# A layer's tail at the end of one DMA stream: x added by a matmul, pieces moved up by one, the last piece cut into 96 and 32 rows

## The chip, the cores and the metric

One core of one Trainium2 chip. The metric is device time in microseconds, the median of several executions. A profile of one execution is shown beside it: engines PE (TensorE), DVE (VectorE), ACT (ScalarE), POOL (GpSimd), SP (SyncE), and the DMA queues.

## The reference

One decode step (batch 2, one token, width 512), float32. The input is normalised once; attention over the last 2048 cached positions with 32 heads of 128, and a bilinear feed-forward block, are both computed from it, and both are added to x.

```python
def _A_ref(x, k_cache, v_cache, wq, wo):      # B, Hq, Dh = 2, 32, 128; W = 2048
    q = (x @ wq) ...                           # per head
    k, v = k_cache[:, :, Sk - W:, :], v_cache[:, :, Sk - W:, :]
    scores = jnp.einsum("bhqd,bhkd->bhqk", q, k) * (Dh ** -0.5)
    p = _softmax(scores, axis=-1)
    o = jnp.einsum("bhqk,bhkd->bhqd", p, v)
    return o.transpose(...).reshape(B, Sq, Hq * Dh) @ wo

def _B_ref(x, w_gate, w_up, w_down):           # F = 1376
    h = (x @ w_gate) * (x @ w_up)
    return h @ w_down

xn = _layernorm(x, axis=-1)
return x + _A_ref(xn, ...) + _B_ref(xn, ...)
```

## The kernel before

All inputs are laid out in one DRAM array, `stream`, in the order in which they are used, and SyncE's DMA queue reads it from front to back. `loads()` is the table of this order. A load is a list of units: `k` and `v` of a head (128 x 4096), `wq` of a group of four heads, `wo` of a head, `wd` a piece of w_down (128 x 512 each: 128 of its 1376 rows, so pieces 0 to 9 are full and piece 10 has 96 rows and is filled up to 128 with zeros). Loads 1 to 22 go into three large buffers in turn (`step0` to `step2`), loads 0 and 23 into `extra`. Load 24 goes into `step0` in separate transfers, so that its units can be used as they land: v 31, wo 28 to 31, then w_down's pieces in three sizes.

A load is issued once the instructions that used its buffer's last content are done; the helper `put` derives these waits from overlapping areas, and `emit` writes all instructions in program order. Every instruction therefore has the line of `emit` in the profile (L199).

For each head VectorE multiplies the keys by q and sums (`score`), for each group of four heads `weights` makes the softmax weights, TensorE weighs the values (`weigh`, into `o_ps`), ScalarE copies them (`fold`), TensorE gathers the diagonal (`gather`, into `pk_ps`, shown as gu), VectorE scales it (`scaled`, into `oT`). The output row is summed in PSUM in two ways. `add_rows` is one matmul of 512 columns into one of four row pairs of `acc`; `add_groups` is four matmuls of 128 columns into `acc_g` (in the bank of q, shown as q). `wo` and `down` use them for wo and w_down; `hT` holds the feed-forward's hidden row, transposed, 128 of its entries a column. `turn` fills it during load 3.

At the end `acc` goes to `acc_sb` in SBUF, and a group of four matmuls with `id4` (a selection matrix: for j = 0 to 3 and b = 0, 1, entry b of row 32j + b is one) adds its four row pairs into `acc_g`. Then `acc_g` is copied to `o_out` and stored. x itself is loaded by ScalarE's DMA queue into two rows of `xr`, which GpSimd has cleared, and VectorE adds it where it copies `acc`.

Of the kernel before, what the change touches and what calls it, by code (L numbers as in the profile page):

```python
# [5 lines left out]
ALU = mybir.AluOpType  # L6
# [4 lines left out]
P = 128  # L11
B, D, H, DH, SK, F = 2, 512, 32, 128, 8192, 1376
# [7 lines left out]
NFC = F // P  # L20
FR = F - NFC * P
# [4 lines left out]
GROUPS = [list(range(g * HG, g * HG + HG)) for g in range(NG)]  # L26
N = B * HG
M = 4 * N
CK, CO = J * DH, D
CX = B * NC + 4 * N + 4 * HG + 2 * NFB + 2 + B  # L30
BUFS = 3
WIDTH = 13824
WIDTH_X = 4096


def loads():


    def units(kind, *ids):
        w = {"k": CK, "v": CK, "wo": CO, "wd": CO, "wq": HG * DH}[kind]  # L40
        return [(kind, i, w) for i in ids]

    def wq(g, *cs):
        return units("wq", *[(g, c) for c in cs])

    big = {
        1: units("k", 0, 1, 2),
        3: units("k", 3, 4) + units("v", 0),
        4: units("k", 5, 6) + units("v", 1),
        5: units("k", 7, 8) + units("v", 2),  # L50
    }
    k, v = 9, 3
    for n in range(6, 20):
        i = 1 + n % 2
        big[n] = units("k", *range(k, k + i)) + units("v", *range(v, v + 3 - i))
        k, v = k + i, v + 3 - i
    big[20] = units("k", 30, 31) + units("v", 24)
    big[21] = units("v", 25, 26, 27)
    big[22] = units("v", 28, 29)
    small = {  # L60
        1: wq(1, 0, 1, 2),
        3: wq(1, 3) + wq(2, 0, 1),
        4: wq(2, 2, 3) + units("wd", 0),
        5: wq(3, 0, 1, 2),
        6: units("wo", 0, 1, 2),
        7: wq(3, 3) + units("wo", 3) + wq(4, 0),
        8: units("wo", 4, 5, 6),
        9: units("wo", 7) + wq(4, 1, 2),
        10: wq(4, 3) + wq(5, 0, 1),
        11: units("wo", 8, 9, 10),  # L70
        12: units("wo", 11) + wq(5, 2, 3),
        13: wq(6, 0, 1, 2),
        14: units("wo", 12, 13, 14),
        15: units("wo", 15) + wq(6, 3) + wq(7, 0),
        16: units("wo", 16, 17, 18),
        17: units("wo", 19) + wq(7, 1, 2),
        18: wq(7, 3) + units("wd", NFC),
        19: units("wo", 20, 21, 22),
        20: units("wo", 23),
        21: units("wo", 26, 27),  # L80
        22: units("wo", 24, 25),
    }
    out = [
        (0, "x", [("c", 0, CX)] + wq(0, 0, 1, 2, 3)),
        (1, 0, big[1] + small[1]),
        (2, 1, [(w, 0, NC * F) for w in ("wg", "wu")]),
        (3, 2, big[3] + small[3]),
    ]
    for n in range(4, 23):
        out += [(n, (1, 0, 2)[(n - 4) % 3], big[n] + small[n])]  # L90
    out += [
        (23, "x", units("v", 30)),
        (24, 0, units("v", 31)),
        (24, 0, units("wo", 28, 29, 30, 31)),
        (24, 0, units("wd", 1, 2, 3, 4)),
        (24, 0, units("wd", 5, 6, 7)),
        (24, 0, units("wd", 8)),
        (24, 0, units("wd", 9)),
    ]
    return out  # L100
# [133 lines left out]
        return call  # L234


def build(nc, stream, x_nat, out):
    pr = Program(nc)
    pe, dve, act, pool = pr.pe, pr.dve, pr.act, pr.pool

    buf = [pr.sb(f"step{i}", [P, WIDTH]) for i in range(BUFS)]
    buf_x = pr.sb("extra", [P, WIDTH_X])
    xr = pr.sb("xr", [P, D])
    ones = pr.sb("ones", [P, P])
    mean_w = pr.sb("mean_w", [P, P])
    eps_t = pr.sb("eps", [P, 1])
    zero = pr.sb("zero", [P, 1])
# [5 lines left out]
    p_all = pr.sb("p", [P, 2, HG, JG, M])  # L253
    s_t = [pr.sb(f"s{i}", [P, HG, J]) for i in range(2)]
    mt = pr.sb("mt", [P, 32])
    mtt = pr.sb("mtt", [P, 32])
    mc = pr.sb("mc", [P, 1])
    both = pr.sb("both", [P, 4 * HG + N])
# [5 lines left out]
    hT = pr.sb("hT", [P, 4, NFB, B])  # L264
    acc_sb = pr.sb("acc_sb", [P, D])
# [4 lines left out]
    acc = pr.ps("acc", [P, FB])  # L270
# [4 lines left out]
    got, used, queue, pos = {}, {}, [], 0  # L275
    for n, t, fields in loads():
        tile = buf_x if t == "x" else buf[t]
        c0 = used.get(n, 0)
        for kind, i, w in fields:
            c = used.get(n, 0)  # L280
            got[kind, i] = tile[:, c : c + w]
            used[n] = c + w
        c1 = used[n]
        assert c1 <= tile.shape[1], (n, c1)
        src = stream[pos : pos + P * (c1 - c0)].rearrange("(p i) -> p i", p=P)
        pos += P * (c1 - c0)
        queue.append((n, tile[:, c0:c1], src))

    def issue(upto):
        while queue and queue[0][0] <= upto:  # L290
# [6 lines left out]
    dve.memset(ones, 1.0)  # L297
    for t in gu_ps + [acc]:
        dve.memset(t, 0.0)
    for t in (xr, zero, mt, both, p_all):  # L300
        pool.memset(t, 0.0)
    pr.load("ACT", xr[:B, :], x_nat)

    c0 = got["c", 0]
    dve.tensor_copy(cst, c0)
# [9 lines left out]
    id4 = cst[:, cut[4] : cut[5]]  # L315
# [82 lines left out]
    def weigh(h, bank=None, first=None, last=None):  # L398
        g, hh = divmod(h, HG)
        bank = g % 2 if bank is None else bank  # L400
        first = hh == 0 if first is None else first
        last = hh == HG - 1 if last is None else last
        v = got["v", h]
        for i in range(JG):
            j = 32 * (i % 4)
            pe.matmul(
                o_ps[bank][j : j + M, :], p_all[:, g % 2, hh, i, :],
                v[:, i * FB : (i + 1) * FB],
                start=(first and i < 4), stop=(last and i >= JG - 4),
            )  # L410
# [58 lines left out]
    def turn():  # L469
        dve.tensor_copy(  # L470
            hT.rearrange("p i n b -> p (i n b)"), hT_ps[:, 0 : 4 * B * NFB]
        )

    def down(c, add, *args, **kw):
        k = min(P, F - c * P)
        add(hT[:k, c % 4, c // 4, :], got["wd", c][:k], *args, **kw)

    def wo(h, add, *args, **kw):
        g, hh = divmod(h, HG)
        add(oT[g % 2][:, B * hh : B * hh + B], got["wo", h], *args, **kw)  # L480

    def keep_busy(lhsT, n):
        pe.matmul(
            spare[:M, : n * P], lhsT, xnb[:, :n, :].rearrange("p c k -> p (c k)"),
            start=True, stop=True,
        )
# [14 lines left out]
    for n, _, fields in loads():  # L501
        plan.setdefault(n, []).extend(fields)
# [19 lines left out]
    for n in range(3, 21):  # L522
# [13 lines left out]
        for c in has(n, "wd"):  # L536
            down(c, add_rows, 1)
# [31 lines left out]
    g = NG - 1  # L569
    a, b, c, d = GROUPS[g]  # L570
# [10 lines left out]
        weigh(h)  # L581
    for h in GROUPS[g - 1]:
        wo(h, add_rows, h % 2)
    weigh(d)
    keep_busy(p_all[:, g % 2, HG - 1, 0, :], 2)
    fold(g)
# [1 line left out]
    scaled(g)  # L588
    for h in GROUPS[g]:
        wo(h, add_rows, h % HG)  # L590
    for i in range(1, 5):
        down(i, add_rows, i % 4, last=True)
    dve.tensor_tensor(acc_sb, acc, xr, op=ALU.add)
    down(5, add_groups)
    add_groups(id4, acc_sb)
    for i in range(6, NFC):
        down(i, add_groups, last=(i == NFC - 1))
    dve.tensor_copy(o_out, acc_g)
    pr.load("SP", out, o_out)
# [3 lines left out]
def laid_out(x):  # L603

    import numpy as np

    a = x["A_x"].reshape(B, D)
    xs = np.zeros((P, CX), a.dtype)
    xs[:, : B * NC] = a.reshape(B, P, NC).transpose(1, 0, 2).reshape(P, B * NC)
    o = B * NC  # L610
    for r in range(4):
        for n in range(N):
            xs[4 * n + r :: 32, o + r * N + n] = 1.0
    o += 4 * N
    for n in range(HG):
        for q in range(4):
            xs[32 * q + n, o + 4 * n + q] = 1.0
    o += 4 * HG
    for n in range(NFB):
        for b in range(B):  # L620
            xs[32 * n + b, o + n * B + b] = 1.0
    o += 2 * NFB
    for j in range(4):
        for b in range(B):
            xs[32 * j + b, o + b] = 1.0
    xs[:, o + 2 :] = a[:, 0]
    cache = {
        kind: x[name][:, :, SK - W :, :].reshape(B, H, HB, J * DH).transpose(1, 0, 2, 3)
        for kind, name in (("k", "A_k_cache"), ("v", "A_v_cache"))
    }  # L630
    wq = x["A_wq"].reshape(P, NC, H * DH)
    wo = x["A_wo"].reshape(H, P, D)
    gu = {
        kind: x[name].reshape(P, NC * F)
        for kind, name in (("wg", "B_w_gate"), ("wu", "B_w_up"))
    }
    wd = x["B_w_down"]

    def field(kind, i):
        if kind == "c":  # L640
            return xs
        if kind in ("k", "v"):
            return cache[kind][i].reshape(P, CK)
        if kind == "wq":
            g, c = i
            return wq[:, c, g * HG * DH : (g + 1) * HG * DH]
        if kind == "wo":
            return wo[i]
        if kind == "wd":
            return np.pad(wd[i * P : (i + 1) * P], ((0, max(0, (i + 1) * P - F)), (0, 0)))  # L650
        return gu[kind]

    parts = [
        np.concatenate([field(kind, i) for kind, i, _ in fields], axis=1).ravel()
        for _, _, fields in loads()
    ]
    return {"stream": np.concatenate(parts), "x": a}


_INS = ["A_x", "A_k_cache", "A_v_cache", "A_wq", "A_wo", "B_w_gate", "B_w_up", "B_w_down"]  # L660
# [24 lines left out]
```

## Time and profile before

| | us |
|---|---|
| median of 3 runs | 377.14 |
| the runs | 376.97 to 377.26 |
| profiled execution | 377.09 |
| its span, first to last instruction | 375.8 |
| VectorE busy | 302.8 (81%) |
| TensorE matmul busy | 191.2 (51%) |
| ScalarE busy | 14.5 (4%) |

The profiled execution's time contains 1.29 us outside its span. Busy shares are averages over the span; the chain of waits, the timeline and the DMA queues say what was waited for at a given place.

### The profile page before, as it was taken

How to read it: one execution, taken by the hardware profiler on the slowest of the kernel's cores; microseconds unless marked ns; L12 is line 12 of the kernel's file. 1: busy time of each engine (PE TensorE's matmuls, PEld its weight loads, DVE VectorE, ACT ScalarE, POOL GpSimd, SP SyncE). 2: the span in 40 equal slices, each digit the busy share in tenths (PEclk: the TensorE clock that was granted, in tenths of full speed). 3: DMA queues.
4: the chain of work that ended last, by engine and by line, in shares of the span. 5: the costliest groups of instructions: out<-in, count | busy, mean ns of one | idle time of the engine just before them, and what ended most of it. 6: DMA issues, size and time to landing. Idle time of an engine off the chain costs nothing.

```text
span 375.8 us, 1953 instructions
## 1 busy us (share of the span) xinstructions
PE 191.2 (51%) x844; PEld 56.9 (15%) x844; DVE 302.8 (81%) x165; ACT 14.5 (4%) x28; POOL 2.6 (1%) x9
## 2 busy tenths in 40 slices
PE   1652646804654265617437263472657355243986
PEld 0210121101210011101121011110111012010322
DVE  4069979999999996999599399969969996999401
ACT  1000100000000000000100000000000001000100
POOL 2000000000000000000000000000000000000000
PEclk9956956676665658758555885856566685565889
DMA  9899989999899998999989999899999999999996
GB/s 398 377 469 413 471 377 471 408 436 466 383 465 418 436 461 383 465 424 430 465 384 459 424 430 465 388 461 418 430 459 414 429 453 434 430 414 411 424 419 242
DMA packets 4475, 159.73 MB, mean 425 GB/s; under 512 B 498, under 2 KB 626, under 8 KB 1012
## 3 DMA queue, kind: packets, MB, share of 16 engines
q1 hardware_dynamic: 4464, 159.62, 98.6%
q8 instruction: 6, 0.10, 0.1%
q14 instruction: 1, 0.01, 0.0%
q10 hardware_dynamic: 4, 0.00, 0.0%
HBM read 159.55 MB, written 0.07 MB: 425 GB/s over the span
## 4 chain that ended last, share of the span: by engine, by line
DVE 49%; DMA 47%; PE 2%; issue 0%; SPq 0%
DMA step<-in_stream_dram 47%; DVE s L199 24%; DVE step L199 23%; PE acc L199 1%; DVE both L199 1%; PE tr L199 1%; PE q L199 0%; SPq L199 0%; DVE mt L199 0%; DVE nm L199 0%; DVE mtt L199 0%; DVE mc L199 0%; DVE rec L199 0%; DVE oT L199 0%; DVE o_out L199 0%
## 5 line engine op out<-in xcount | busy, mean ns | idle before, releaser
L199 DVE TENSOR_TENSOR step<-step,q 128x4096 f32<-128x4096 f32 x32 | 141.1, 4409 | 38.0 <-DMA step<-in_stream_dram 37.9
L199 DVE TENSOR_REDUCE s<-step 128x32 f32<-128x4096 f32 x32 | 141.4, 4418 | 0.8
L199 PE MATMUL o_ps<-step,p 128*32 128x512 f32 x496 | 101.2, 923 | 68.1 <-DMA step<-in_stream_dram 66.5
L199 PE MATMUL q<-step,xnb 128*128 128x512 f32 x56 | 37.5, 801 | 28.7 <-DVE step L199 21.7
L199 PE MATMUL acc<-step,oT 128*2 128x512 f32 x64 | 23.5, 922 | 40.7 <-DVE oT L199 27.0
L199 PEld LDWEIGHTS o_ps<-step,p 128*32 128x32 f32 x496 | 21.2, 154 | 130.2 <-DMA step<-in_stream_dram 74.0
L199 PEld LDWEIGHTS q<-step,xnb 128*128 128x128 f32 x56 | 12.5, 251 | 55.0 <-DVE step L199 28.2
L199 ACT ACTIVATE p<-s,zero 64x128 f32<-64x128 f32 x16 | 6.4, 399 | 266.2 <-DVE s L199 266.1
L199 PE MATMUL tr<-both,ones 128*128 128x24 f32 (+1 forms) x18 | 4.7, 344 | 19.7 <-DVE both L199 19.7
L199 DVE TENSOR_TENSOR oT<-gu,rec 128x8 f32<-128x8 f32 x8 | 1.3, 159 | 14.8 <-PE gu L199 14.8
L199 PE MATMUL gu<-step,xn 128*2 128x512 f32 (+1 forms) x48 | 8.7, 659 | 7.5 <-DMA step<-in_stream_dram 7.5
L199 PE MATMUL gu<-cst,o_sb 128*128 128x8 f32 x64 | 10.1, 285 | 3.1 <-ACT o_sb L199 3.1
L199 PEld LDWEIGHTS gu<-cst,o_sb 128*128 128x128 f32 x64 | 9.4, 225 | 10.8 <-ACT o_sb L199 9.1
L199 PEld LDWEIGHTS acc<-step,oT 128*2 128x2 f32 x64 | 1.5, 82 | 51.5 <-DVE oT L199 27.7
L199 PEld LDWEIGHTS tr<-both,ones 128*128 128x128 f32 x18 | 3.7, 256 | 29.2 <-DVE both L199 29.2
L199 PE MATMUL q<-extra,xnb 128*128 128x512 f32 x8 | 6.4, 978 | 1.9 <-DVE xnb L199 1.9
L199 DVE TENSOR_REDUCE nm<-tr 64x4 f32<-64x8 f32 x16 | 2.6, 163 | 5.2 <-PE tr L199 5.1
L199 ACT COPY o_sb<-o_ps 128x512 f32<-128x512 f32 x8 | 4.7, 586 | 48.2 <-PE o_ps L199 48.2
L199 PE MATMUL gu<-cst,h_sb 128*128 128x6 f32 x8 | 1.9, 361 | 5.4 <-DVE h_sb L199 5.4
L199 PEld LDWEIGHTS gu<-step,xn 128*2 128x2 f32 x48 | 2.0, 93 | 14.9 <-DMA step<-in_stream_dram 9.1
L199 PE MATMUL tr<-st,mean_w 128*128 128x4 f32 x2 | 0.6, 366 | 6.5 <-DVE st L199 6.5
L199 DVE TENSOR_REDUCE both<-p 128x8 f32<-128x256 f32 x8 | 3.3, 414 | 0.6 <-ACT p L199 0.6
(50 smaller groups left out, 39.3 us busy)
## 6 DMA issues: line engine op xcount, KB each, us to landing
step<-in_stream_dram SPq DMA_DIRECT2D x17, 6912.0 KB, 31.3
step<-in_stream_dram SPq DMA_DIRECT2D x2, 6656.0 KB, 33.6
step<-in_stream_dram SPq DMA_DIRECT2D x1, 6400.0 KB, 29.5
step<-in_stream_dram SPq DMA_DIRECT2D x1, 5504.0 KB, 33.4
step<-in_stream_dram SPq DMA_DIRECT2D x1, 4608.0 KB, 23.8
extra<-in_stream_dram SPq DMA_DIRECT2D x1, 2048.0 KB, 28.3
step<-in_stream_dram SPq DMA_DIRECT2D x1, 2048.0 KB, 24.8
step<-in_stream_dram SPq DMA_DIRECT2D x2, 1024.0 KB, 19.6
```

Source lines behind the costliest of these rows:

```text
L199: ins = getattr(e, method)(*args, **kw)
```

## The change

x is no longer loaded by itself. Its two rows are stored in piece 10 of w_down, as rows 96 and 97 of the 128, and two rows of a unit matrix (from `id4`) are copied behind the 96 hidden entries in `hT`; the matmul of piece 10, now with 98 rows, adds x. `xr`, its memset, its load and its input are gone. `acc` is copied by ScalarE instead of added to by VectorE.

Piece 1 of w_down moves into load 22 and is used between the matmuls of wo for heads 24 and 25; load 24 has pieces 2 to 5 in one transfer, 6 and 7 in one, then 8, then 9. Pieces 2 to 5 are added by rows, 6 to 9 by groups, and the group with `acc_sb` comes behind piece 7 instead of piece 5.

Piece 9 is loaded in two transfers: rows 0 to 95, and rows 96 to 127 as four blocks of eight rows. In `stream` a row of padding is stored behind each block, so that the four blocks are a dimension of their own.

```diff
+LAST, LAST_K = 32, 4
...
-        22: units("wo", 24, 25),
+        22: units("wo", 24, 25) + units("wd", 1),
...
-        (24, 0, units("wd", 1, 2, 3, 4)),
-        (24, 0, units("wd", 5, 6, 7)),
+        (24, 0, units("wd", 2, 3, 4, 5)),
+        (24, 0, units("wd", 6, 7)),
         (24, 0, units("wd", 8)),
         (24, 0, units("wd", 9)),
...
-    xr = pr.sb("xr", [P, D])
...
+        if fields[0][:2] == ("wd", NFC - 1):
+            k, lo, j = LAST_K, P - LAST, LAST // LAST_K
+            src = stream[pos : pos + lo * CO].rearrange("(p i) -> p i", p=lo)
+            queue.append((n, tile[:lo, c0:c1], src))
+            pos += lo * CO
+            src = stream[pos : pos + k * (j + 1) * CO].rearrange(
+                "(i j d) -> i j d", i=k, d=CO
+            )
+            queue.append((n, tile[lo:, c0:c1], src[:, :j, :]))
+        else:
+            queue.append((n, tile[:, c0:c1], src))
         pos += P * (c1 - c0)
-        queue.append((n, tile[:, c0:c1], src))
...
-    for t in (xr, zero, mt, both, p_all):
+    for t in (zero, mt, both, p_all):
         pool.memset(t, 0.0)
-    pr.load("ACT", xr[:B, :], x_nat)
...
         )
+        dve.tensor_copy(hT[FR : FR + B, NFC % 4, NFC // 4, :], id4[FR : FR + B, :])
 
     def down(c, add, *args, **kw):
-        k = min(P, F - c * P)
+        k = min(P, F + B - c * P)
...
     for h in GROUPS[g - 1]:
         wo(h, add_rows, h % 2)
+        if h == GROUPS[g - 1][0]:
+            down(1, add_rows, 2)
...
-    for i in range(1, 5):
+    for i in range(2, 6):
         down(i, add_rows, i % 4, last=True)
-    dve.tensor_tensor(acc_sb, acc, xr, op=ALU.add)
-    down(5, add_groups)
+    act.copy(acc_sb, acc)
+    for i in (6, 7):
+        down(i, add_groups)
     add_groups(id4, acc_sb)
-    for i in range(6, NFC):
+    for i in range(8, NFC):
         down(i, add_groups, last=(i == NFC - 1))
```

TensorE's last instructions before the change, from the matmuls of wo's last four heads on; `s_d567` to `s_d571` are the landings of load 24's transfers behind v 31.

```order
L199 MATMUL acc<-step,oT 2x512 [waits s_d567,s_DVE]
L199 MATMUL acc<-step,oT 2x512 x3
L199 MATMUL acc<-step,hT 2x512 [waits s_d568]
L199 MATMUL acc<-step,hT 2x512 x3
L199 MATMUL q<-step,hT 2x128 [waits s_d569]
L199 MATMUL q<-step,hT 2x128 x3
L199 MATMUL q<-acc_sb,cst 2x128 [waits s_DVE]
L199 MATMUL q<-acc_sb,cst 2x128 x3
L199 MATMUL q<-step,hT 2x128 x8
L199 MATMUL q<-step,hT 2x128 [waits s_d570]
L199 MATMUL q<-step,hT 2x128 x3
L199 MATMUL q<-step,hT 2x128 [waits s_d571]
```

The same place after the change; here `s_d566` to `s_d571` are the landings.

```order
L200 MATMUL acc<-step,oT 2x512 [waits s_d566,s_DVE]
L200 MATMUL acc<-step,oT 2x512 x3
L200 MATMUL acc<-step,hT 2x512 [waits s_d567]
L200 MATMUL acc<-step,hT 2x512 x3
L200 MATMUL q<-step,hT 2x128 [waits s_d568]
L200 MATMUL q<-step,hT 2x128 x7
L200 MATMUL q<-acc_sb,cst 2x128 [waits s_ACT]
L200 MATMUL q<-acc_sb,cst 2x128 x3
L200 MATMUL q<-step,hT 2x128 [waits s_d569]
L200 MATMUL q<-step,hT 2x128 x3
L200 MATMUL q<-step,hT 2x128 [waits s_d570,s_d571]
```

The group with `acc_sb` now waits for ScalarE and stands behind two groups of `hT` instead of one; three groups of w_down stand ahead of the last piece instead of four, and the last piece waits for two landings.

SyncE's last transfers before the change.

```order
L199 DMA step<-in_stream_dram 128x9216 [waits s_DVE]
L199 DMA extra<-in_stream_dram 128x4096
L199 DMA step<-in_stream_dram 128x4096 [waits s_DVE]
L199 DMA step<-in_stream_dram 128x2048 [waits s_DVE]
L199 DMA step<-in_stream_dram 128x2048
L199 DMA step<-in_stream_dram 128x1536 [waits s_PE]
L199 DMA step<-in_stream_dram 128x512 [waits s_PE] x2
L199 DMA out_dram<-o_out 128x128 [waits s_DVE]
```

And after it.

```order
L200 DMA step<-in_stream_dram 128x9728 [waits s_DVE]
L200 DMA extra<-in_stream_dram 128x4096
L200 DMA step<-in_stream_dram 128x4096 [waits s_DVE]
L200 DMA step<-in_stream_dram 128x2048 [waits s_DVE]
L200 DMA step<-in_stream_dram 128x2048
L200 DMA step<-in_stream_dram 128x1024 [waits s_PE]
L200 DMA step<-in_stream_dram 128x512 [waits s_PE]
L200 DMA step<-in_stream_dram 96x512 [waits s_PE]
L200 DMA step<-in_stream_dram 32x1x512
L200 DMA out_dram<-o_out 128x128 [waits s_DVE]
```

Load 22 (the first row) has grown by 512 columns and the transfer of three pieces has lost as many; the last row of 128x512 has become one of 96 and one of 32 rows.

More of the change, by code (lines that the diff above doesn't have):

```diff
@@ L234, in __getattr__, with build @@
         return call
-def build(nc, stream, x_nat, out):
+def build(nc, stream, out):
     pr = Program(nc)
@@ L649, in field @@
         if kind == "wd":
-            return np.pad(wd[i * P : (i + 1) * P], ((0, max(0, (i + 1) * P - F)), (0, 0)))
+            rows = np.zeros((P, D), wd.dtype)
+            rows[: min(P, F - i * P)] = wd[i * P : (i + 1) * P]
+            if i == NFC:
+                rows[FR : FR + B] = a
+            return rows
         return gu[kind]
@@ L656, in laid_out @@
     ]
-    return {"stream": np.concatenate(parts), "x": a}
+    last = wd[NFC * P - LAST : NFC * P].reshape(LAST_K, LAST // LAST_K, D)
+    parts.append(parts.pop()[: -LAST * D])
+    parts.append(np.pad(last, ((0, 0), (0, 1), (0, 0))).ravel())
+    return {"stream": np.concatenate(parts)}
 _INS = ["A_x", "A_k_cache", "A_v_cache", "A_wq", "A_wo", "B_w_gate", "B_w_up", "B_w_down"]
```

## The prediction

> **What bounds the kernel now.** I read the page first: its span, the line of DMA shares, the DMA queues.
>
> ```profile
> span 375.8 us, 1953 instructions
> ...
> DMA  9899989999899998999989999899999999999996
> ...
> q1 hardware_dynamic: 4464, 159.62, 98.6%
> q8 instruction: 6, 0.10, 0.1%
> q14 instruction: 1, 0.01, 0.0%
> q10 hardware_dynamic: 4, 0.00, 0.0%
> HBM read 159.55 MB, written 0.07 MB: 425 GB/s over the span
> ```
>
> SyncE's queue q1 takes 98.6% of the sixteen DMA engines' time, and only the last slice falls to 6 tenths. The stream of inputs is the bound from first to last, at 425 GB/s, or 425/16 = 26.6 GB/s on one DMA engine. So an edit counts if it changes the bytes, leaves the stream dry, or touches what lies behind its end. The packet counts also say how a transfer is cut: 31 transfers on q1 give 4464 = 31 x 144, which is 128 rows and 16 closing packets each. The load of x on q10, two rows, made 4 packets: two rows and two closings, so it ran on two engines only.
>
> Next the chain of waits at its end, and the timeline of the last 11 us.
>
> ```profile
> 350.06 22.00 DMA step<-in_stream_dram
> 372.10 1.27 PE q L199 x40
> 373.38 0.44 PE q L199 x8
> 373.85 0.29 DVE o_out L199
> ```
>
> ```profile
> 365.26 1.92 PE L199 MATMUL o_ps<-step,p 128*32 128x512 f32 x16 [1.02 <-DMA step<-in_stream_dram]
> ...
> 367.25 0.59 ACT L199 COPY o_sb<-o_ps 128x512 f32<-128x512 f32 x1 [14.01 <-PE o_ps L199]
> ...
> 368.98 0.17 DVE L199 TENSOR_TENSOR oT<-gu,rec 128x8 f32<-128x8 f32 x1 [14.14 <-PE gu L199]
> 369.20 0.11 PEld L199 LDWEIGHTS acc<-step,oT 128*2 128x2 f32 x8 [0.35 <-DVE oT L199]
> 369.20 1.04 PE L199 MATMUL acc<-step,oT 128*2 128x512 f32 x8 [0.26 <-DVE oT L199]
> ...
> 370.24 1.04 PE L199 MATMUL acc<-step,hT 128*2 128x512 f32 x8
> 371.34 0.69 DVE L199 TENSOR_TENSOR acc_sb<-acc,xr 128x512 f32<-128x512 f32 x1 [2.20 <-PE acc L199]
> 372.10 0.11 PEld L199 LDWEIGHTS q<-step,hT 128*2 128x2 f32 x8 [1.76 <-DMA step<-in_stream_dram]
> 372.10 0.40 PE L199 MATMUL q<-step,hT 128*2 128x128 f32 x8 [0.83 <-DMA step<-in_stream_dram]
> ...
> 372.32 0.40 PE L199 MATMUL q<-acc_sb,cst 128*2 128x128 f32 x8
> ...
> 372.54 1.25 PE L199 MATMUL q<-step,hT 128*2 128x128 f32 x32
> 373.38 0.11 PEld L199 LDWEIGHTS q<-step,hT 128*2 128x2 f32 x8 [0.30 <-DMA step<-in_stream_dram]
> ...
> 374.17 0.35 SPq L199 DMA_DIRECT2D out_dram<-o_out  x1
> ```
>
> The last eight matmuls (piece 9) start at 373.38 after a wait of 0.30 us for their DMA. Behind them lie 0.44 us of matmul, 0.29 us of copy and the store, none of which the change touches. In the run before them one group of eight starts each 0.22 us (372.10, 372.32, 372.54), so TensorE would have been ready for the last at about 372.10 + 5 x 0.22 = 373.2: the landing leads by some 0.2 us.
>
> Last, the final stretch of the DMA in narrow windows.
>
> ```profile
> core 0: us, PE busy (x) PEld busy (x) DVE busy (x) ACT busy (x) POOL busy (x), PEclk, DMA share, GB/s
> ...
> 370.00:371.00 1.00, 1.00 (x12) 0.11 (x8) 0.00 (x0) 0.00 (x0) 0.00 (x0) 1.00 1.00 391
> 371.00:371.50 0.50, 0.28 (x4) 0.00 (x0) 0.16 (x1) 0.00 (x0) 0.00 (x0) 1.00 0.67 258
> 371.50:372.00 0.50, 0.00 (x0) 0.00 (x0) 0.50 (x1) 0.00 (x0) 0.00 (x0) 1.00 0.45 172
> 372.00:372.50 0.50, 0.40 (x16) 0.39 (x20) 0.04 (x1) 0.00 (x0) 0.00 (x0) 1.00 0.40 152
> 372.50:373.00 0.50, 0.50 (x29) 0.48 (x24) 0.00 (x0) 0.00 (x0) 0.00 (x0) 1.00 0.17 66
> ```
>
> The engines do not end together. The share is 1.00 until 371.0, then 0.45 of sixteen, which is seven engines, and these run dry between about 372.2 and 373.0. Nine engines are done by 371.5, the last piece waits for the other seven, and seven is also the number of program fetches on q8 and q14 (6 + 1). One of them, by itself in its window, shows the price:
>
> ```profile
> q8 instruction: 1, 0.02, 3.1%
> ```
>
> That is 3.1% of sixteen engines over the 2.1 us from 66.5 to 68.6, or 1.04 us of one engine. An engine that fetched program once is about that late at the end.
>
> **The change part by part.**
>
> *The last piece.* At 370 to 371 us, where the short pieces run at full share, an engine moves 391/16 = 24.4 GB/s, so one row of 2 KB costs it 2048 B / 24.4 GB/s = 0.084 us. Before, each engine had eight rows of piece 9; now it has six, which is 2 x 0.084 = 0.17 us less on the engines that end last. Four engines get 32/4 = 8 rows more: 14 instead of eight, 6 x 0.084 = +0.50 us. An engine done by 371.5 is then done by 372.0, still ahead of the late ones. If all four are early ones the last landing moves by -0.17 us; if one of them is the latest of all it moves by +0.50 us. These are the two ends. That the small part runs on four engines follows from its source, four blocks of eight rows, as the two rows of x ran on two. It is issued with the last pieces:
>
> ```profile
> step<-in_stream_dram SPq DMA_DIRECT2D x17, 6912.0 KB, 31.3
> ...
> step<-in_stream_dram SPq DMA_DIRECT2D x2, 256.0 KB, 22.3
> ```
>
> These are issued 22.3 us before they land, so one more transfer on SyncE's queue, 0.35 us by the row of the store at 374.17, is hidden; only the store is behind it, 22 us later.
>
> [...]
>
> *The wait for two landings.* The last group now waits for two semaphores. The row of oT shows such a wait: it ends at 368.98 + 0.17 = 369.15 and TensorE, which waits there for wo's landing too, starts at 369.20. In the new place the wait served first can be the one that ends last, so the matmul is dispatched behind it. Ends: 0 us, and 0.30 us, the idle time in the row at 373.38. I take 0.05 us, the row of oT being the same kind of wait.
>
> *x by matmul.* Two more rows of piece 10, which was filled up to 128 rows already: no byte more. The matmul of 96 rows becomes one of 98 at unchanged width:
>
> ```profile
> L199 PE MATMUL acc<-step,hT x12: 591/592/592, 73.8 to 370.7; 128*2 128x512 f32 x10, 96*2 96x512 f32 x2
> ...
> L199 DVE COPY hT<-gu x1: 175/175/175, 55.7 to 55.7; 128x24 f32<-128x24 f32 x1
> ```
>
> With 96 and with 128 rows it takes 591 to 592 ns, so the two rows cost nothing. VectorE gets one copy of 2x2 elements behind the copy of hT, at most its 0.175 us. A transfer of 6912 KB takes 7.08 MB / 425 GB/s = 16.7 us and lands 31.3 us after issue, so loads queue some 15 us ahead; that cover hides 0.175 us, uncovered it would be 0.175 us. Gone are the load of x and a memset, which lie here:
>
> ```profile
> 0.73 0.52 POOL L199 MEMSET xr<- 128x512 f32 x1 [0.29 <-POOLq L669]
> ...
> 1.28 0.52 ACTq L199 DMA_DIRECT2D xr<-in_x_dram  x1
> ...
> 5.67 0.20 DVE L199 COPY cst<-extra 128x66 f32<-128x66 f32 x1 [2.86 <-DMA extra<-in_stream_dram]
> ```
>
> The first arithmetic waits until 5.67 us for the first piece of the stream, so what goes before 2 us gains nothing; the two rows of x give two engines back 0.08 us each, a gain only on a late one.
>
> *ScalarE's copy for VectorE's add.* 0.69 us becomes a copy of the kind at 367.25, 0.59 us. It isn't on the path: see the next sum.
>
> *Pieces one up.* w_down's piece 1 rides in load 22; v 30, v 31, wo 28 to 31 and the piece of four now land 256 KB later, 262144 B / 425 GB/s = 0.62 us. The pieces of two, 8 and 9 end at the same byte as before. TensorE's tail moves: the weighing waited for v 31 at 365.26, now 365.88; the four wo matmuls end at 370.24 + 0.62 = 370.86; the piece of four lands about then; its matmuls end at 371.34 + 0.62 = 371.96; ScalarE's copy ends at 372.55. In place of one group TensorE now does pieces 6 and 7 first, 372.10 to 372.54, then acc_sb's group at about 372.6, piece 8 at 372.8, and is ready for piece 9 at 373.05. Its landing, with the 0.17 us taken off, lets it start at 373.38 - 0.17 = 373.21: still last. Piece 1's own matmul, about 0.5 us, goes ahead of the wait of 1.02 us at 365.26 and into it.
>
> Sum, on the profiled execution of 377.09 us (span 375.8, 1.29 around it): -0.17 + 0.05 = -0.12, 376.97 us. That execution is 0.05 us under the median of 377.14 (runs from 376.97 to 377.26), so I say 377.0 us. 0.2% is 0.75 us, about what a measurement of this kernel can tell from no change.
>
> **The rivals.**
>
> *A late engine among the four.* The trace does not number engines. For it: seven of sixteen are late; four drawn blindly would all be early 1 time in 14 (9/16 x 8/15 x 7/14 x 6/13 = 0.07). Against: seven fetches made seven engines late, none twice, so engines are taken in turn, and a run of neighbours can leave the four wholly out. Price: an engine with 14 rows sets the end once it is late to within 0.50 + 0.17 = 0.67 us of the last, which most of the seven are (the last window still holds 66/26.6 = 2.5 engines on the mean). The time is 376.97 plus at most 0.67, 377.64 us, slower than before; for one in the middle of the seven about 377.3 us. [...]
>
> *The 96 rows gain nothing.* The late engines' six rows may take as long as eight did, if what they write to is the limit and not the engine: 377.09 + 0.05 = 377.14 us. For it: the rows give an engine's rate, not the side that limits it. Against: 0.45 and 0.40 of the engines in the windows carry 172 and 152 GB/s, 23.9 and 23.8 GB/s for each; at full share it was 24.4, so engines are not held back by their neighbours. [...]
>
> *ScalarE's copy comes late.* If the copy ends 0.16 us or more later than reckoned, acc_sb's group and with it piece 9 starts after the landing; at 0.5 us late the piece starts at 373.55 for 373.38, 377.09 + 0.17 = 377.26 us. Against it, the margin of 373.21 - 373.05 = 0.16 us above, and shifts that only follow the stream.
>
> *One more program fetch.* With other instruction counts a fetch may fall on an engine that is late already: 1.04 us more, 378.1 us, slower by over 0.2%. TensorE loses some matmuls and VectorE's count hardly moves, which speaks against.
>
> **How the numbers follow.** Forecast, four early engines: 0.45. Late engine: 0.35. No gain: 0.10. Late copy: 0.05. Fetch or something like it: 0.05. The range reaches from the whole 0.17 us at the distance of the fastest run from the median, 0.17 us more (377.09 - 0.17 - 0.17 = 376.75), to the late engine's worst, 377.64. Only the fetch leaves the 0.75 us upwards, and a little of the late engine with the wait's 0.30 us: slower 0.06. Downwards no term reaches 0.75 us, 0.03 for what I overlook. Same: 0.91.
>
> **What would show it.** The page after should count 4320 + 112 + 36 = 4468 packets on q1, and no q10. Right: piece 9's wait ends about 0.17 us nearer to that of piece 8. Wrong: the last window of DMA holds one to four engines for 0.4 us longer (late engine), the last groups wait for ScalarE (late copy), or q8 and q14 hold eight fetches.

## The result, and the profile after

The changed kernel takes 377.74 us (median of 20 runs, 377.49 to 378.15) against 377.12 us before (20 runs, 376.95 to 377.35): 1.0016 times the time, 95% interval 1.001 to 1.0023. It is 0.62 us slower and lies 0.10 us above the stated range (377.64); the forecast was 0.1 us faster. The profiled execution took 377.91 us.

The page after, its span and DMA queues:

```profile
span 376.6 us, 1941 instructions
...
q1 hardware_dynamic: 4468, 159.62, 98.5%
q8 instruction: 6, 0.10, 0.1%
q14 instruction: 1, 0.01, 0.0%
HBM read 159.55 MB, written 0.07 MB: 424 GB/s over the span
```

The same bytes and the same seven program fetches; 4468 packets say that the 32 rows did run on four engines, and q10 is gone. The chain's end and TensorE's tail, where before the waits ended at 372.10 and 373.38:

```profile
350.19 22.82 DMA step<-in_stream_dram
373.06 1.05 PE q L200 x32
374.19 0.44 PE q L200 x8
374.65 0.29 DVE o_out L200
```

```profile
366.04 1.92 PE L200 MATMUL o_ps<-step,p 128*32 128x512 f32 x16 [1.03 <-DMA step<-in_stream_dram]
...
371.08 1.04 PE L200 MATMUL acc<-step,hT 128*2 128x512 f32 x8
372.19 0.59 ACT L200 COPY acc_sb<-acc 128x512 f32<-128x512 f32 x1 [3.57 <-PE acc L200]
373.06 0.33 PEld L200 LDWEIGHTS q<-step,hT 128*2 128x2 f32 x16 [1.87 <-DMA step<-in_stream_dram]
...
374.15 0.14 PEld L200 LDWEIGHTS q<-step,hT 128*2 128x2 f32 x8 [0.34 <-DMA step<-in_stream_dram]
```

Up to the copy, which ends at 372.78, everything is where it was reckoned, 0.2 us later. But TensorE then waits until 373.06 for pieces 6 and 7. Their bytes end in the stream where those of pieces 5 to 7 ended before, and that wait ended at 372.10. The loss of 0.96 us is there already, ahead of piece 9. The windows of the end say what kind of loss:

```profile
370.00:371.00 1.00, 1.00 (x8) 0.10 (x8) 0.00 (x0) 0.00 (x0) 0.00 (x0) 1.00 1.00 356
371.00:371.50 0.50, 0.45 (x8) 0.11 (x8) 0.00 (x0) 0.00 (x0) 0.00 (x0) 1.00 0.80 172
371.50:372.00 0.50, 0.50 (x8) 0.00 (x0) 0.00 (x0) 0.00 (x0) 0.00 (x0) 1.00 0.68 201
372.00:372.50 0.50, 0.12 (x4) 0.00 (x0) 0.00 (x0) 0.31 (x1) 0.00 (x0) 1.00 0.61 193
372.50:373.00 0.50, 0.00 (x0) 0.00 (x0) 0.00 (x0) 0.28 (x1) 0.00 (x0) 1.00 0.42 119
373.00:373.50 0.50, 0.44 (x17) 0.42 (x21) 0.00 (x0) 0.00 (x0) 0.00 (x0) 1.00 0.24 86
```

The last two columns are the share of sixteen DMA engines that was busy, and GB/s. Before, 0.67 of the engines moved 258 GB/s from 371.0 to 371.5, 24 GB/s each. Now 0.80 of them move 172, which is 172 / (0.80 x 16) = 13.4 GB/s each. More engines are busy and each is slower, from the time when the early engines reach the 96 and 32 rows: the first of them landed piece 8 at 370.86 us. The single rows in the trace say the same: a row of 2 KB that began between 371.0 and 371.5 took 0.086 us before and 0.161 us now (medians).

### The profile page after: what moved, and what is told of

It is laid out like the page before. It is cut to its first block, busy times and chain, and to the rows that moved or that the text cites. A ratio compares the mean times of both kernels' runs of the same rounds, so it can differ in the third digit from the quotient of the medians.

```text
span 376.6 us, 1941 instructions
## 1 busy us (share of the span) xinstructions
PE 185.6 (49%) x838; PEld 55.0 (15%) x838; DVE 302.3 (80%) x165; ACT 15.1 (4%) x29; POOL 2.2 (1%) x8
## 3 DMA queue, kind: packets, MB, share of 16 engines
q1 hardware_dynamic: 4468, 159.62, 98.5%
## 4 chain that ended last, share of the span: by engine, by line
DVE 49%; DMA 48%; PE 2%; issue 1%; SPq 0%
DMA step<-in_stream_dram 48%; DVE s L200 24%; DVE step L200 23%; PE acc L200 1%; DVE both L200 1%; PE tr L200 1%; SPq L200 0%; PE q L200 0%; DVE mt L200 0%; DVE nm L200 0%; DVE mtt L200 0%; DVE mc L200 0%; DVE rec L200 0%; DVE oT L200 0%; DVE o_out L200 0%
## 5 line engine op out<-in xcount | busy, mean ns | idle before, releaser
L200 PE MATMUL o_ps<-step,p 128*32 128x512 f32 x496 | 99.2, 905 | 71.8 <-DMA step<-in_stream_dram 70.2
L200 PE MATMUL q<-step,xnb 128*128 128x512 f32 x56 | 36.4, 781 | 31.2 <-DVE step L200 22.7
L200 PE MATMUL acc<-step,oT 128*2 128x512 f32 x64 | 22.7, 883 | 41.5 <-DVE oT L200 27.0
L200 PE MATMUL q<-extra,xnb 128*128 128x512 f32 x8 | 5.2, 809 | 1.9 <-DVE xnb L200 1.9
L200 PE MATMUL acc<-step,hT 128*2 128x512 f32 (+1 forms) x14 | 4.1, 592 | 0.1
## 6 DMA issues: line engine op xcount, KB each, us to landing
step<-in_stream_dram SPq DMA_DIRECT2D x1, 4864.0 KB, 24.4
```

The source lines that it names most:

```text
L200: ins = getattr(e, method)(*args, **kw)
```

## The experiments

Three theories stood at the start. P: rows of the two new transfers slow engines that are at work at the same time, also those that are still at older rows (13.4 GB/s each for 24 is the reading it starts from). E: one of the four engines with 14 rows is a late one. M: the moved pieces, the copy or the matmul of x cost it.

**One transfer again.** The change without its last part:

```diff
-        if fields[0][:2] == ("wd", NFC - 1):
-            ...
-        else:
-            queue.append((n, tile[:, c0:c1], src))
+        queue.append((n, tile[:, c0:c1], src))
```

> The changed kernel, but piece 9 is one transfer of 128 rows again (x by matmul, ScalarE's copy and the moved pieces stay). [...] Theory M (the moved pieces or the copy cost it): stays at 377.7 us.

Measured: 377.08 us, ratio to before 0.9998 (0.9989 to 1.0007). Its windows are those of before:

```profile
371.00:371.50 0.50, 0.50 (x8) 0.09 (x8) 0.00 (x0) 0.00 (x0) 0.00 (x0) 1.00 0.62 238
371.50:372.00 0.50, 0.50 (x8) 0.00 (x0) 0.00 (x0) 0.00 (x0) 0.00 (x0) 1.00 0.45 172
```

24.0 and 23.9 GB/s for each busy engine. M falls: x by matmul, ScalarE's copy and the moved pieces together cost nothing that can be measured, and gain nothing.

**The split alone.** The kernel before with only piece 9's two transfers (the same lines of the diff, put into the kernel before).

> The kernel before, with nothing of the change but piece 9 in 96 and 32 rows on four engines. P and E: 377.7 us, the whole loss. M: 377.1 us. Under P the transfer of three pieces ahead of it lands late too (after 372.5 instead of 372.06), under E only piece 9 does.

Measured: 377.85 us, 1.0018 (1.0009 to 1.0027), the whole loss. The group behind the transfer of pieces 5 to 7 starts at 372.79 instead of 372.10:

```profile
372.79 0.11 PEld L200 LDWEIGHTS q<-step,hT 128*2 128x2 f32 x8 [2.42 <-DMA step<-in_stream_dram]
```

So a transfer of 128 rows that lies ahead in the stream is late, as P said.

**Both parts on sixteen engines.** In the change:

```diff
...
-            src = stream[pos : pos + k * (j + 1) * CO].rearrange(
-                "(i j d) -> i j d", i=k, d=CO
-            )
-            queue.append((n, tile[lo:, c0:c1], src[:, :j, :]))
+            src = stream[pos : pos + LAST * CO].rearrange("(p i) -> p i", p=LAST)
+            queue.append((n, tile[lo:, c0:c1], src))
...
```

> The changed kernel with piece 9 in 96 and 32 rows, both on sixteen engines (six rows and two rows each, so each engine again has eight). E: no engine has more than before, 377.1 us. [...]

Measured: 377.77 us, 1.0018 (1.001 to 1.0027). No engine has more bytes than before, and the loss stays:

```profile
371.00:371.50 0.50, 0.50 (x8) 0.02 (x5) 0.00 (x0) 0.00 (x0) 0.00 (x0) 1.00 0.93 213
371.50:372.00 0.50, 0.45 (x8) 0.00 (x0) 0.00 (x0) 0.00 (x0) 0.00 (x0) 1.00 0.53 123
```

14.3 and 14.5 GB/s for each busy engine.

**The same bytes per engine, cut by columns.**

```diff
...
-            src = stream[pos : pos + lo * CO].rearrange("(p i) -> p i", p=lo)
-            queue.append((n, tile[:lo, c0:c1], src))
+            src = stream[pos : pos + P * w].rearrange("(p i) -> p i", p=P)   # w = 384
+            queue.append((n, tile[:, c0 : c0 + w], src))
...
-            queue.append((n, tile[lo:, c0:c1], src[:, :j, :]))
+            queue.append((n, tile[:, c0 + w : c1], src[:, :j, :]))           # j = 32 rows of 512 B
...
```

> The changed kernel with piece 9 cut by columns: 384 columns of all 128 rows on sixteen engines, 128 columns on four engines as 32 rows of 512 B each. Bytes per engine are those of the change (12 KB, and 16 KB more on four), but the sixteen-engine part has 128 rows. E: as slow as the change or slower, 377.6 to 378 us. P: only the four engines meet others, so the piece of two lands near 372.1 to 372.4 and the time is 377.0 to 377.4 us.

Measured: 377.09 us, 1.0 (0.9992 to 1.0009).

```profile
371.00:371.50 0.50, 0.50 (x8) 0.00 (x0) 0.00 (x0) 0.00 (x0) 0.00 (x0) 1.00 0.64 229
371.50:372.00 0.50, 0.32 (x4) 0.00 (x0) 0.00 (x0) 0.11 (x1) 0.00 (x0) 1.00 0.63 224
```

```profile
q1 hardware_dynamic: 4596, 159.62, 98.7%
```

22.4 and 22.2 GB/s. The packet count on the page is 30 x 144 + 144 + 128 + 4 = 4596, so the last 128 rows ran on four engines, and these four had as many bytes more as in the change. E falls as the cause. The trace also has the time at which each engine of a transfer landed. In the change three of the four engines landed their eight rows at 373.07 to 373.21 us and the fourth, a late one, at 373.88; the last engine of the 96 rows landed behind it, at 374.05. So one late engine was among the four, as E supposes, and it still did not set the end.

But the late engines had a quarter less of piece 9 here, and the time is the one of the undivided piece (377.08 us): the gain of 0.17 us that the prediction counted on did not show either, within 0.1%.

**The price by itself.** One load in the middle of the stream (load 10, in the kernel before) was cut in four ways, with no byte more; the first is a control, and S is the rival that a second transfer costs something fixed whatever its rows:

```diff
+        if n == 10:
+            for lo, hi in ((0, 96), (96, 128)):      # or (0, 64), (64, 128); or (32, 96), (0, 32), (96, 128)
+                queue.append((n, tile[lo:hi, c0:c1], src[lo:hi, :]))
+        else:
+            queue.append((n, tile[:, c0:c1], src))
```

The control cuts `c0` to `c1` at the middle instead of the rows.

> Control: the same load cut into two halves of columns, 128 rows each. P and S: 377.1 us, within 0.3.

> The same load cut into rows 0 to 63 and 64 to 127. [...] S: 377.1 us.

> The same load cut into rows 32 to 95, 0 to 31 and 96 to 127. [...] Rival R (any transfer with fewer than 128 rows is slow by itself): as slow as the cut into halves or slower.

> The kernel before, with one load in the middle of the stream (load 10, 128 rows of 55 KB, 16.3 us) cut into rows 0 to 95 and 96 to 127, both on sixteen engines; no byte more. A row takes an engine 2.04 us. [...] Rival S (a second transfer or short ends cost something fixed, only visible at the end of the stream): within 0.5 us of 377.1.

| load 10 cut into | us | ratio (95%) |
|---|---|---|
| two halves of columns | 377.22 | 1.0002 (0.9993 to 1.0012) |
| rows 0 to 63, 64 to 127 | 397.48 | 1.0542 (1.0521 to 1.0562) |
| rows 32 to 95, 0 to 31, 96 to 127 | 387.76 | 1.0282 (1.0267 to 1.0297) |
| rows 0 to 95, 96 to 127 | 396.23 | 1.0508 (1.0493 to 1.0524) |

Windows of that load: the kernel before, the halves, the middle 64 rows first (two windows: those rows, then the two quarters), and the cut at row 96.

```profile
150.00:156.00 6.00, 5.11 (x20) 1.46 (x21) 5.09 (x2) 0.00 (x0) 0.00 (x0) 0.63 1.02 442
```

```profile
152.00:180.00 28.00, 6.39 (x22) 1.72 (x22) 17.59 (x4) 0.00 (x0) 0.00 (x0) 0.62 1.04 215
```

```profile
150.00:156.00 6.00, 5.07 (x19) 1.18 (x20) 5.05 (x2) 0.00 (x0) 0.00 (x0) 0.54 1.04 442
158.00:172.00 14.00, 0.00 (x0) 0.00 (x0) 10.54 (x3) 0.00 (x0) 0.00 (x0) 0.66 0.91 190
```

```profile
152.00:180.00 28.00, 6.01 (x22) 1.66 (x22) 17.59 (x4) 0.00 (x0) 0.00 (x0) 0.62 1.04 217
```

64 rows ran at 442 GB/s when they were rows 32 to 95, as 128 rows did, and at 215 GB/s when they were 0 to 63 and 64 to 127. The single rows of 55 KB in the trace say it more sharply: 2.0 to 2.1 us for a row in the kernel before and among rows 32 to 95, 4.1 to 4.3 us in the cut into halves. Both cuts read 64 neighbouring rows of `stream` at a time, so the reading side does not tell them apart. Size and number of transfers are not the cause (rival S and rival R fall); which rows travel together is. Why it is these rows, no run shows. The halves cost 20.4 us and the middle cut 10.6, in both cases more than I had estimated: a row in the halves takes a little more than twice as long, up to 4.3 us for 2.04, and the two quarters together ran at 190 GB/s. The cut at row 96 cost 19 us, also more than my estimate. All its rows ran at about half rate: of the rows that began between 151 and 172 us none took less than 3.9 us.

**One pair, and the whole transfer's pace.** The cut at 36 instead of 32 was to show whether slow engines hold up the rest of their transfer. The line taken away is that of the cut into rows 32 to 95, 0 to 31 and 96 to 127.

```diff
-            for lo, hi in ((32, 96), (0, 32), (96, 128)):
+            for lo, hi in ((36, 100), (0, 36), (100, 128)):
```

> The kernel before, with load 10 cut into rows 36 to 99, 0 to 35 and 100 to 127. [...]

Measured: 403.04 us, 1.0689 (1.0658 to 1.072). The total says little here, since the two rests did not run on sixteen engines: the 4490 packets on the page are 30 x 144 + 80 + 36 + 12 + 28 + 14, which fits 36 rows on twelve engines and 28 on fourteen. The first 64 rows were to answer the question:

```profile
150.00:158.00 8.00, 5.59 (x19) 1.40 (x20) 5.58 (x2) 0.00 (x0) 0.00 (x0) 0.50 0.91 332
152.00:156.00 4.00, 3.59 (x17) 1.02 (x18) 3.61 (x1) 0.00 (x0) 0.00 (x0) 0.50 1.07 415
```

Over the 8 us behind 150 us it is 332 GB/s, between the 442 of rows 32 to 95 and the 215 of the halves; the inner 4 us show 415. With rows of 55 KB such short windows are coarse, so they leave it open. The single rows in the trace decide. Of those that began between 151 and 153 us eleven took 2.2 us, two 2.6 and two 4.3. Two engines landed these 64 rows at 167.4 and 167.7 us, the fourteen others by 163.8. So two engines went at about half pace, and the rest of their transfer was not held to it. What made the first row of most engines slow too (about 3.5 us) stays open; it may be why the 8 us stay under 415.

**96 rows from another start.** Load 10 once more, and piece 9 of the changed kernel with its 96 rows from row 32:

```diff
-            for lo, hi in ((32, 96), (0, 32), (96, 128)):
+            for lo, hi in ((32, 128), (0, 32)):
```

```diff
...
-            queue.append((n, tile[:lo, c0:c1], src))
+            queue.append((n, tile[LAST:, c0:c1], src))
...
-            queue.append((n, tile[lo:, c0:c1], src[:, :j, :]))
+            queue.append((n, tile[:LAST, c0:c1], src[:, :j, :]))
...
```

> The kernel before, with load 10 cut into rows 32 to 127 and 0 to 31, both on sixteen engines. [...] Theory Q (96 rows are handed out as 64 and then 32, four and two neighbouring rows an engine): rows 32 to 95 at full rate, so some 440 GB/s from 150 to 156 us, then the rest at half rate, about 387 us as with the middle 64 cut out. Theory C (six neighbouring rows an engine) or T (three times 32 rows, two an engine): as slow from its start as the cut at row 96, 150 to 156 us at about 200 to 300 GB/s, 390 to 396 us.

> The changed kernel with piece 9 cut the other way: 96 rows from row 32 on sixteen engines, rows 0 to 31 on four. Engines have the same bytes as in the change. Q: four of the six rows of an engine are clear of the others, less of the loss stays, 377.1 to 377.5 us. C or T: the same loss as the change, 377.6 to 377.9 us. Theory E (only the bytes on a late one of the four engines count) says 377.7 us too, but the four-engine part by columns, with the same bytes, has already shown 377.09 us.

Measured: 396.71 us, 1.0519 (1.05 to 1.0538), and 377.66 us, 1.0012 (1.0003 to 1.0021). In the cut load the stretch that ran at 442 GB/s for rows 32 to 95 is slow from its start, with the same 166 GB/s as in the cut at row 96:

```profile
150.00:156.00 6.00, 3.24 (x16) 0.87 (x17) 3.26 (x1) 0.00 (x0) 0.00 (x0) 0.50 0.80 166
```

My theory Q, that 96 rows begin with 64 at full rate, fell: from 151 to 172 us every row took 4.1 to 4.4 us. C and T expect the same of these two runs, and nothing here shows the rows of an engine, so which of them holds, if either, stays open. For the change it is enough: the load with a transfer of 96 rows ran at about half rate from row 0 and from row 32 (217 GB/s from 152 to 180 us in both cuts, 442 for the whole load), and engines still at work on older rows were slowed (the transfer of three pieces in the split alone, used from 372.79 instead of 372.10).

**What makes engines late.** The prediction took seven late engines for seven program fetches.

```diff
-        for i in range(JG):
+        for i in range(4 if first or last else 0):
...
-                start=(first and i < 4), stop=(last and i >= JG - 4),
+                start=first, stop=last,
```

> The kernel before without most of the weighing of the values (for the first and last head of each group four of eight matmuls are left, for the others none; the output lacks their part), which takes 768 of TensorE's 1688 instructions away; all transfers are unchanged. If a program fetch makes one engine late and there is about one for each 256 TensorE instructions, q8 shows three fetches in place of six, and in the window from 371.5 to 372.0 four engines are still busy (0.25 and some 95 GB/s) in place of seven (0.45 and 172 GB/s). The time stays near 377.0 us, since one late engine is enough to hold the last piece. If the lateness has another cause, the window stays at seven engines.

This kernel leaves out most of the weighing of the values. The program fetches on its page, and two windows:

```profile
q8 instruction: 3, 0.05, 0.1%
q14 instruction: 1, 0.01, 0.0%
```

```profile
371.50:372.00 0.50, 0.50 (x8) 0.10 (x4) 0.00 (x0) 0.00 (x0) 0.00 (x0) 0.50 0.29 111
372.00:372.50 0.50, 0.50 (x8) 0.05 (x4) 0.00 (x0) 0.00 (x0) 0.00 (x0) 0.50 0.21 82
```

Three fetches on q8 with one on q14, and 0.29 of sixteen, 4.6 engines, where 0.45 or 7 had been busy; 0.21 or 3.4 in the next window, before 0.40 or 6.4. Fewer fetches left fewer late engines, and the rest are late as before. The engines' own landings show it one by one. In the kernel before, one of sixteen engines lands 0.7 us or more behind the others after the fetch at 67 us, two after the fetch at 89, three after 141, four after 191, five after 253, six after 317 and seven after 359, and piece 9 lands on nine engines by 371.93 and on seven from 372.63 to 373.34. In this run eleven engines land piece 9 by 371.97 and five later, one more than there are fetches; one engine lay 0.3 us behind the others from the first load on. The reading holds.

The time did not stay: 377.03 to 379.65 us over eight runs, median 378.61, ratio 1.0028 (1.0005 to 1.005). The column before the DMA share is TensorE's granted clock: 0.50 at this place, where it was 1.00 in the kernel before. In the profiled execution, one of the longer ones (379.02 us), the eight matmuls of wo took 1.89 us in place of 1.04, and piece 9 waited for TensorE and no longer for its landing. So the total of this run says nothing on the late engines.

## Why the prediction was wrong

*The last piece* is the step that failed. Its price of a row, 0.084 us at 24.4 GB/s an engine, was taken from transfers of 128 rows and applied to 96 and 32 rows, beside which the engines ran slower: 13.4 GB/s for a busy engine in the changed kernel, 14.3 and 14.5 with both parts on sixteen engines, and 215 to 217 GB/s in place of 442 where a whole load is cut so. Instead of -0.17 us the term is +0.66 us (change 377.74, the same without the split 377.08). I had bounded it by 14 rows on the latest engine, +0.50 us; that a transfer could slow others that are ahead of it in the stream was not in the sum at all, and that is where 0.96 us were lost before piece 9 began.

*The rivals.* "The 96 rows gain nothing" had the right place but the wrong price: it ends at 377.14 us, no shorter than before, and the change lost 0.62 us. I spoke against it with windows in which every transfer had 128 rows, 24 GB/s an engine, and concluded that engines are not held back by their neighbours; such windows cannot show what 96 and 32 rows do, which was 13.4. Its chance was 0.10. "A late engine among the four" (0.35) would have ended on the right side, and one of the four was late, but it landed ahead of the last of the 96 rows, and cut by columns the same bytes on four engines, one of them late, cost nothing (377.09 us). The sign that I had named for it was there too (0.24 of sixteen, 3.8 engines, still busy from 373.0 to 373.5); engines slowed by the split leave the same sign. The fetch and the late copy did not occur: seven fetches as before, and ScalarE's copy ended 0.28 us ahead of the wait that mattered.

*What held.* x by matmul, the copy and the moved pieces cost nothing (ratio 0.9998). The shift of 0.62 us in the tail came as 0.78 us: v 31's group at 366.04 for 365.88. The packet count was 4468. One engine more was late for each program fetch, seven for seven in the kernel before.

*The gain of 0.17 us* does not show in the times even without the loss: 377.09 us by columns, 377.08 us in one piece. In the two profiled executions it is there in part: the last engine of piece 9 landed 1.15 us behind the last of pieces 6 and 7 when cut by columns (372.05 to 373.20), and 1.28 us behind in one piece (372.18 to 373.46). There the late one of the four engines landed at 373.18, just ahead of the last. What takes the 0.13 us in the other executions stays open. None of the versions beats the kernel before.

## What to carry to other kernels

If a DMA transfer has to be cut, try columns before rows: here a load cut into halves of its rows or at row 96 ran at 215 to 217 GB/s in place of 442 (rows 32 to 95 kept 442), and a split at the end also slowed an older transfer, used from 372.79 instead of 372.10 us, while cuts by columns cost nothing (1.0002, 1.0). The rate per engine read here from 128-row transfers, 24.4 GB/s, did not hold for 96 and 32 rows (13.4); before moving bytes between engines, look which rows travel at the same time. At the end of a stream, see GB/s and busy share together: here a falling share with full GB/s per busy engine (24) was a stagger, and a high share with about half of it (13.4) was engines slowed by the split.

## What the runs showed of the hardware

Rows 32 to 95 of the load, a transfer of 64, ran at 442 GB/s like the whole load; in two halves, 0 to 63 and 64 to 127, the load ran at 215 GB/s. Cut into 96 and 32 rows it ran at 217 GB/s, with the 96 from row 0 and from row 32. With rows 36 to 99, two engines took 4.3 us for a row of 55 KB that takes 2.04 us in the kernel before, and fourteen engines landed by 163.8 us, before those two at 167.4 and 167.7. In the kernel before, each program fetch left one more of the sixteen engines late, 0.7 us or more, to the end of the stream, seven after seven; with four fetches five were late, one of them by 0.3 us from the first load on. Cutting one load out of some thirty into halves or at 96 rows cost 19 to 20 us, 5% of the kernel; cut by columns, it cost nothing (1.0002).
